# Decode attention over a 4096-token window: K and V in 4 MB slabs of 32 KB rows, five slots, in place of 2 MB slabs of 16 KB rows, eight slots

## The chip, the core and the metric

The kernel runs on one NeuronCore of a Trainium2 chip; the other cores are idle. The metric is the device time of one execution in microseconds (us). The profile adds, for one execution, the span from the first to the last instruction; it is about 2 us shorter than the measured time. Runs are called fast or slow by their state; only fast runs are compared, unless the text says otherwise. Ratios are the mean time of one kernel's fast runs over that of the other's of the same rounds, so they are not quite the ratio of the medians quoted beside them.

PE is the matmul engine, PEld its weight loads, DVE the vector engine, ACT the scalar engine, POOL the general engine, SP the engine that issues nearly all loads here. "Idle DMA" below is the time in which one of the core's 16 DMA engines has no packet, averaged over the 16; I summed it from the packet records of the trace, where each packet has a start, a duration and a size.

## The reference

Two independent problems A and B with the same shapes. One new token per batch attends to the last 4096 positions of a cache; two query heads share one kv head.

```python
B, Sq, D = 2, 1, 576
Hq, Hkv, Sk, Dh = 32, 16, 16384, 128
W = 4096
q = (x @ wq)                                   # wq: 576 x 4096
k = k_cache[:, :, Sk - W:, :]                  # each kv head serves 2 query heads
v = v_cache[:, :, Sk - W:, :]
p = softmax(einsum("bhqd,bhkd->bhqk", q, k) * Dh**-0.5)
o = einsum("bhqk,bhkd->bhqd", p, v)
out = o.reshape(B, 1, 4096) @ wo               # wo: 4096 x 576
# the outputs of A and B are joined along the last axis
```

All data are bf16. K and V windows are 134 MB, wq and wo 19 MB more, so 153 MB are read once.

## The kernel before

A slab is one kv head of both batches: 64 rows of 64 tokens for each batch, 128 partitions, 16 KB per partition, 2 MB. K and V slabs go through one ring of eight slots. SP issues all loads in one fixed order, the stream; it waits for each slot (or buffer) to be free, and everything behind waits too.

```python
NR = 8          # slots
LAG = 7         # V slab i stands behind K slab i + 7
for t in range(NSLAB + LAG):                      # NSLAB = 32
    if t < NSLAB:
        stream.append(("K", t))
    if t >= LAG:
        i = t - LAG
        if i % 4 == 0 and i // 4 < NG - 1:
            stream.append(("W", i // 4))          # a block of wo, 1.2 MB
        stream.append(("V", i))
stream.append(("W", NG - 1))
...
    # issue of a wo block: two buffers, so it waits for the projection before the last
    deps = [proj_op[i - 2]] if i >= 2 else []
```

For each K slab, DVE transposes 32x32 blocks (`xt`), then PE makes scores with a masked, shifted q as weights (`zq`). The scores of four slabs share two PSUM banks, so one softmax serves four slabs (eight softmaxes in all). The order of an iteration, which is the program order on each engine:

```python
make_X(t, 0); make_S(t, 0)        # DVE transpose of half a slab, 8 score matmuls on PE
make_chain(Gc)                    # every 4th t: max, transpose of it, bias, 4 exps
make_dg(Gp)                       # every 4th t: pick the diagonal of the PV product
make_X(t, 1); make_S(t, 1)
make_A(Gp); make_chain2(Gc); make_rl(Gp)
make_PV(i)                        # 16 matmuls, two 32-column tiles of PE at a time
make_chain3(Gc); make_evac(...)   # 1/sum, PSUM -> SBUF with that scale
make_proj(Gp)                     # times wo, summed in PSUM
...
```

## Time and profile before

| | before |
|---|---|
| time, median of the first three runs | 368.95 us (368.38 to 369.19) |
| span in the profile | 366.6 us |
| first packet / last data packet ends | 1.8 us / 363.3 us |
| idle DMA between | 1.8 us, 0.8 of it up to 345 us |
| PE, DVE busy | 74%, 51% |

From the page of the kernel before: the span, the busy times, the two rows of the 40 slices that concern the DMA (busy tenths, then GB/s), the packet sum, and four groups of instructions (busy us, mean ns of one, idle time before and its releaser). L437 is the transpose, L585 the PV product.

```profile
span 366.6 us, 3694 instructions
PE 271.8 (74%) x1700; PEld 101.0 (28%) x1435; DVE 185.9 (51%) x189; ACT 34.3 (9%) x114; POOL 14.1 (4%) x53
...
DMA  8999999999999999999999999999999999999994
GB/s 322 447 408 427 429 429 423 432 426 427 429 431 427 427 427 426 426 427 428 424 428 431 427 426 429 431 426 429 429 419 429 429 429 429 421 428 429 425 415 183
DMA packets 11264, 153.34 MB, mean 418 GB/s; under 512 B 1256, under 2 KB 1392, under 8 KB 2032
...
L437 DVE STREAM_TRANSPOSE xt<-ring 128x2048 f32<-128x2048 f32 x64 | 144.5, 2287 | 91.3 <-DMA ring<-in_A_k_cache_dram 46.7
...
L585 PE MATMUL ot<-ring,pT 128*32 128x512 bf16 x448 | 55.1, 395 | 0.7 <-ACT oE L610 0.7
...
ring<-in_A_v_cache_dram SPq DMA_DIRECT2D x16, 2048.0 KB, 35.8
...
wob<-in_A_wo_dram SPq DMA_DIRECT2D x4, 1152.0 KB, 33.5
```

The DMA engines are busy in every slice but the first and the last. A K or V load lands 33 to 37 us after SP issues it (medians of the page), because some 15 MB of loads are queued ahead of it. DVE idles for want of K. So this kernel is a stream of 153 MB with a short start and tail.

The queue's own waits (who SP waited for: us in total, times, longest) show that SP is blocked most of the time:

```profile
SPq L373 <- DVE xt L437: 133.4, 31, 8.1
SPq L373 <- PE ot L585: 45.4, 13, 4.5
SPq L347 <- PE pj L683: 43.5, 5, 10.4
```

L373 is the issue of a K or V slab, L347 that of a wo block, `pj` the projection.

### The profile page before, as it was taken

Reading aid. Unit: us, or ns where it says so; the run is one execution under the profiler, and the core shown is the slowest. Engines: PE = TensorE matmul, PEld = TensorE weight load, DVE = VectorE, ACT = ScalarE, POOL = GpSimd, SP = SyncE. Lnnn points to the kernel's source line nnn. Section 1 sums busy time; section 2 is a strip of 40 time slices with the busy share of each in tenths; the row PEclk is TensorE's granted clock in tenths of the full one; section 3 lists DMA queues with packets and bytes.
Section 4 is the critical chain, followed back from the end, with each engine's and each line's share of the span. In section 5 each row is a group of like instructions: output and inputs, shape, how many; then the busy total and the mean of one; then the engine's idle time right before and its main releaser. Section 6 shows DMA issues by size and latency. Waiting matters only on the chain.

```text
span 366.6 us, 3694 instructions
## 1 busy us (share of the span) xinstructions
PE 271.8 (74%) x1700; PEld 101.0 (28%) x1435; DVE 185.9 (51%) x189; ACT 34.3 (9%) x114; POOL 14.1 (4%) x53
## 2 busy tenths in 40 slices
PE   0635975987679788567968876794996677498797
PEld 0311112122214322132314321151223222143554
DVE  3104997967543674435744584407745476233100
ACT  1011002002000110002000020001200030002100
POOL 5010000000000000000000000000000000000000
PEclk9976897698985889895895998867798989958958
DMA  8999999999999999999999999999999999999994
GB/s 322 447 408 427 429 429 423 432 426 427 429 431 427 427 427 426 426 427 428 424 428 431 427 426 429 431 426 429 429 419 429 429 429 429 421 428 429 425 415 183
DMA packets 11264, 153.34 MB, mean 418 GB/s; under 512 B 1256, under 2 KB 1392, under 8 KB 2032
## 3 DMA queue, kind: packets, MB, share of 16 engines
q1 hardware_dynamic: 11236, 153.10, 98.6%
q8 instruction: 12, 0.20, 0.2%
q14 instruction: 4, 0.03, 0.0%
q10 hardware_dynamic: 12, 0.01, 0.0%
HBM read 153.10 MB, written 0.00 MB: 418 GB/s over the span
## 4 chain that ended last, share of the span: by engine, by line
DMA 82%; DVE 13%; PE 4%; SPq 0%; issue 0%
DMA ring<-in_B_k_cache_dram 41%; DMA ring<-in_A_k_cache_dram 28%; DVE xt L437 12%; DMA ring<-in_B_v_cache_dram 10%; DMA ring<-in_A_wq_dram 4%; PE ot L274 1%; PE st L461 1%; PE st L381 1%; PE pj L683 0%; PE st L395 0%; SPq L373 0%; PE st L594 0%; SPq L368 0%; DVE out_sb L693 0%; DVE ssum L536 0%
## 5 line engine op out<-in xcount | busy, mean ns | idle before, releaser
L437 DVE STREAM_TRANSPOSE xt<-ring 128x2048 f32<-128x2048 f32 x64 | 144.5, 2287 | 91.3 <-DMA ring<-in_A_k_cache_dram 46.7
L461 PE MATMUL st<-xt,zq 128*128 128x512 bf16 x256 | 115.6, 452 | 62.6 <-DVE xt L437 62.5
L381 PE MATMUL st<-xt,zq 128*128 128x512 bf16 x256 | 115.6, 451 | 0.0
L461 PEld LDWEIGHTS st<-xt,zq 128*128 128x128 bf16 x256 | 28.4, 111 | 158.8 <-DVE xt L437 82.7
L585 PE MATMUL ot<-ring,pT 128*32 128x512 bf16 x448 | 55.1, 395 | 0.7 <-ACT oE L610 0.7
L585 PEld LDWEIGHTS ot<-ring,pT 128*32 128x32 bf16 x448 | 20.5, 100 | 33.8 <-issue 15.4
L620 PEld LDWEIGHTS tb<-selv,oE 128*128 128x128 f32 x112 | 21.1, 280 | 5.8 <-issue 4.0
L620 PE MATMUL tb<-selv,oE 128*128 128x16 f32 x112 | 19.8, 324 | 0.8 <-ACT oE L610 0.8
L424 POOL TENSOR_TENSOR zq<-qs,bmask 128x64 bf16<-128x64 bf16 x32 | 9.2, 292 | 270.5 <-PE st L381 177.9
L639 DVE TENSOR_TENSOR oA<-tb,cmask 128x256 bf16<-128x256 f32 x7 | 3.0, 425 | 29.1 <-PE tb L620 29.1
L610 ACT ACTIVATE oE<-ot,rsb 128x512 f32<-128x512 f32 x14 | 9.6, 685 | 84.2 <-PE ot L585 84.2
L512 ACT ACTIVATE pR<-st,bias_sb 128x256 bf16<-128x256 f32 x32 | 15.9, 545 | 0.3
L471 DVE TENSOR_REDUCE mx<-st 128x2 f32<-128x512 f32 x16 | 10.0, 664 | 3.0 <-PE tb L651 3.0
L683 PE MATMUL pj<-wob,oP 128*2 128x288 bf16 x126 | 10.9, 324 | 0.3 <-ACT oP L655 0.3
L531 DVE STREAM_TRANSPOSE pT<-pR 128x512 bf16<-128x512 bf16 x16 | 10.4, 685 | 0.0
L501 PE MATMUL tb<-ones_f,nMrep 1*128 1x1 f32 x32 | 5.6, 276 | 6.0 <-DVE nMrep L495 6.0
L505 ACT ACTIVATE bias_sb<-tb 128x2 f32<-128x2 f32 x8 | 1.4, 172 | 89.1 <-PE tb L501 89.1
L255 PE MATMUL tb<-ident_b,xt 2*128 2x2 bf16 x36 | 2.3, 194 | 9.9 <-DVE xt L222 9.9
L655 ACT ACTIVATE oP<-tb 128x16 bf16<-128x16 f32 x8 | 1.5, 191 | 86.8 <-PE tb L651 86.8
L594 PEld LDWEIGHTS st<-pT,ring 128*128 128x128 bf16 x256 | 7.4, 102 | 5.1 <-DMA ring<-in_B_v_cache_dram 4.9
L594 PE MATMUL st<-pT,ring 128*128 128x16 bf16 x256 | 7.7, 173 | 0.5 <-DMA ring<-in_B_v_cache_dram 0.4
L631 DVE TENSOR_TENSOR oA<-st,cmr 128x64 bf16<-128x64 f32 x4 | 0.9, 225 | 13.7 <-PE st L594 13.7
(67 smaller groups left out, 92.7 us busy)
## 6 DMA issues: line engine op xcount, KB each, us to landing
ring<-in_A_k_cache_dram SPq DMA_DIRECT2D x16, 2048.0 KB, 33.2
ring<-in_A_v_cache_dram SPq DMA_DIRECT2D x16, 2048.0 KB, 35.8
ring<-in_B_k_cache_dram SPq DMA_DIRECT2D x16, 2048.0 KB, 37.1
ring<-in_B_v_cache_dram SPq DMA_DIRECT2D x15, 2048.0 KB, 36.9
ring<-in_A_wq_dram SPq DMA_DIRECT2D x1, 4608.0 KB, 13.8
ring<-in_B_wq_dram SPq DMA_DIRECT2D x1, 4608.0 KB, 24.3
wob<-in_A_wo_dram SPq DMA_DIRECT2D x4, 1152.0 KB, 33.5
wob<-in_B_wo_dram SPq DMA_DIRECT2D x3, 1152.0 KB, 30.8
```

What stands on the lines that cost most here:

```text
L381: return e.add_instruction(mybir.InstMatmult(name=nc.get_next_instruction_name(), engine=mybir.EngineType.PE, ins=[e.lower_ap(mv), e.lower ...
L424: return e.tensor_tensor(dst, src, msk, ALU.mult)
L437: Xop[(t, jb)] = S.add("dve", lambda e: e.transpose(xt[:, n % NXT, :].bitcast(FP32), ring[:, r, jb * HW_:(jb + 1) * HW_].bitcast(FP32)), d ...
L461: last = e.matmul(st[bk][:, 0:512], wt, mv, start=first, stop=True, skip_group_check=True)
L471: mxs = [S.add("dve", lambda e, jb=jb: e.tensor_reduce(mx[:, jb, :], st[jb][:, :].rearrange("p (x t) -> p t x", t=2), AX.X, ALU.max), [Sop ...
L512: last = e.activation(pR[:, jb, :].rearrange("p (x t) -> p t x", t=2)[:, t, :], st[jb][:, :].rearrange("p (x t) -> p t x", t=2)[:, t, :], ...
L531: chain[(G, "pT%d" % jb)] = S.add("dve", lambda e, jb=jb: e.transpose(pT[:, v, 512 * jb:512 * jb + 512].rearrange("p (w j q) -> p j w q", ...
L585: last = e.matmul(OTB[32 * c:32 * c + 32, :], pT[:, v, col:col + 32], ring[:, r, j * 128:(j + 4) * 128], start=(j % 32 == 0), stop=(j % 32 ...
L594: last = e.matmul(OL[m % 2][:, 0:16], ring[:, r, j * 128:(j + 1) * 128], pT[:, v, col:col + 16], start=(j == 0), stop=(j == KR - 1))
L610: evac_op[(G, pr)] = S.add("act", lambda e: e.activation(oE[:, pr, :], OTB[:, :], ACTF.Copy, scale=rsb[:, v, pr:pr + 1]), deps, "oE%d_%d" ...
L620: last = e.matmul(bank[:, 0:16], oE[:, pr, 128 * c:128 * c + 128], selv[:, pr, c, :], start=(pr == 0 and c == 0), stop=(pr == 1 and c == 3))
L683: last = e.matmul(PJ[half], oP[:, v, j, :], wob[:, v, j, half * NH:(half + 1) * NH], start=(proj_start(G) and j == 0), stop=True, skip_gro ...
```

## The change

Its intent is longer rows: a slab becomes four kv heads of one batch, interleaved on the partitions, 32 rows of 128 tokens each, so 32 KB per partition and half as many packets. A ring of five such slots takes 20 MB instead of 16, and only one wo buffer is kept. Each slab now holds 8 query rows by itself, so each has its own softmax, with four biases (one per kv head); PV uses all four column tiles of PE. The diff, cut to what matters:

```diff
-    NR = 8
-    NXT = 3
+    NR = 5
+    NXT = 5
-    LAG = 7
+    LAG = 2
-    KR = W // 64
+    KR = W // 32
-        wob = sb("wob", [128, 2, 8, NOUT], BF16)
+        wob = sb("wob", [128, 8, NOUT], BF16)
...
-                if i % 4 == 0 and i // 4 < NG - 1:
-                    stream.append(("W", i // 4))
+                if i % 2 == 1 and i // 2 < NSG - 1:
+                    stream.append(("W", i // 2))
                 stream.append(("V", i))
...
-                deps = [proj_op[i - 2]] if i >= 2 else []
+                deps = [proj_op[i - 1]] if i >= 1 else [q_free]
...
-            src = src_t[:, g, Sk - W:Sk, :].rearrange("b (r j) d -> r b (j d)", j=KR)
+            src = src_t[b, 4 * G:4 * G + 4, Sk - W:Sk, :].rearrange("g (r j) d -> r g (j d)", j=KR)
...
-                    for t in range(2):
-                        last = e.activation(pR[:, jb, :].rearrange("p (x t) -> p t x", t=2)[:, t, :], ...
+                    for t in range(4):
+                        last = e.activation(pR[:, bk, :].rearrange("p (x t) -> p t x", t=4)[:, t, :], ...
...
+                    for k in range(8):
+                        bk, jq = k // 4, k % 4
+                        for z in range(4):
+                            last = e.matmul(OTB[32 * z:32 * z + 32, :], pT[:, v, col:col + 32], ...
```

The iteration after the change, in program order (t is the K slab, c = t - 1 the slab whose softmax runs, i = t - 2 the slab whose PV runs, d = t - 3 the slab that is finished; `chain1` to `chain4` are the pieces of one softmax, and `dg`, `A` and `rl` pick the wanted part of a PV product and lay it out for the projection):

```python
make_X(t, 0); make_X(t, 1); make_S(t, 0)
chain1(c); make_X(t, 2); chain2(c); make_X(t, 3); make_S(t, 1)
make_dg(d); make_X(t, 4); make_X(t, 5); make_S(t, 2)
chain3(c); make_A(d)
if d % 2 == 1: make_rl(d // 2)
make_X(t, 6); chain4(c); make_X(t, 7); make_S(t, 3)
if d % 2 == 1: make_proj(d // 2)     # behind all 32 score matmuls of slab t
make_PV(i); make_evac(i)
```

## The prediction

> **What bounds it now.** The DMA stream. The page's slices show 16 busy DMA engines and 419 to 431 GB/s in nearly every slice between the start and the tail; 153.1 MB pass in about 358.4 us (first packet at 1.8 us, V cache landed near 360 us). The rest is a tail of some 6 us. PE is 74% busy, DVE 51%: both wait for data. The queue's own waits show SP blocked most of the time, but each load lands 33 to 37 us after issue, so some 15 MB are always queued and nothing starves.
>
> **What the change gives.** The packet records of the trace fit one line: 16 KB rows take 613 ns, 36 KB rows (wq) 1364 ns, 9.2 KB rows 352 ns, which is 436 GB/s over 16 engines plus about 12 ns per packet. This agrees with the Trainium skill, "DMA: Bandwidth & Descriptors", section "Where 436 GB/s comes from" (435 GB/s fabric ceiling). 32 KB rows halve the K/V packets: about 10,000 packets become about 6,000, so 4,000 x 12.2 ns / 16 = 3.0 us off the stream; the fewer completion writes give 0.2 us. PV on four column tiles shortens PE work (now 1.9 us per 2 MB slab), which is off the critical path. Start and tail keep their lengths. Best case: about 365.7 us, 1% faster.
>
> **What it adds.** Softmax runs 16 times, not 8, with eight short exps (estimate 0.37 us pitch from 0.475 us for twice the columns) and transposes of half the size (estimate 1.17 us each from a 2.24 us pitch). DVE grows by an estimated 35 to 40 us, still under 70%; this alone doesn't bind.
>
> **What I think binds.** wo now has one buffer, not two. The load of wo block n waits for projection n-1, and SP issues in order. That projection stands after all scores of the K slab that landed last but with only one V and one K slab queued behind it: 2 x 9.7 us = 19.4 us of cover. From landing to the end of that projection I chain, with durations of the trace: two transposes 2.4; scores 1.95 at full clock (3.4 to 3.9 at half); maximum transpose, nM, nMrep 0.9; next transpose 1.2; scores 1.95; dg 1.5; scores 1.95; row-sum transpose, ssum, rc, rs 1.2; last transpose 1.2; scores 1.95; projection 1.2: about 17.6 us at full clock. Issue to first data (1.0 to 1.2 us, seen at the start) and landing to consumer (0.5 us) leave no slack. PE has then been idle over 5 us. By the Trainium skill, "TensorE: Matmul & The Clock Gate", section "What's actually happening", an idle PE falls to half clock; the trace agrees (eight score matmuls take 1.75 or 3.39 us). With a cold first group the projection ends at 19.5 to 20.5 us: a bubble of about 1.8 to 2.8 us. It occurs six times (blocks 1 to 6): estimate 11 us in all, 0 to 20.
>
> **Prediction.** 368.95 - 3.2 + 11 = about 377 us; 80% range 366 to 387. Faster by over 2%: 3%; within 2%: 43%; slower by over 2%: 54%.
>
> **What would show it.** Right: K/V packets of about 1214 ns; DMA slices near 431 GB/s, with six dips some 43 us apart; in the queue's waits SP at the wo load waiting for the projection, and little else. Wrong: no dips (the stream alone, about 365 us); dips at K or V loads (compute loop too long); PV still 0.11 us per matmul.
>
> **What would make it wrong.** PE staying at full clock, or a shorter softmax chain, hides the wait; a colder PE (each score group +1.5 us) doubles it; 32 KB packets may not follow the line.

## The result, and the profile after

The changed kernel took 384.44 us (382.78 to 386.04, six runs) against 368.74 us for the kernel before in the same rounds: ratio 1.0423, 95% interval 1.0394 to 1.0452. It is 4% slower.

From the page of the changed kernel, the lines that answer to those above (L431 is the transpose, L552 the PV product, L491 the exps):

```profile
span 382.5 us, 3829 instructions
PE 238.2 (62%) x1613; PEld 89.5 (23%) x1353; DVE 218.1 (57%) x331; ACT 71.8 (19%) x322; POOL 9.7 (3%) x33
...
DMA  8999999999997999999997999769998999969994
GB/s 347 432 427 437 435 425 432 416 437 435 432 399 298 428 422 427 371 448 433 432 433 312 434 439 435 339 235 439 439 439 336 413 422 433 439 261 462 428 394 192
DMA packets 6802, 153.35 MB, mean 401 GB/s; under 512 B 760, under 2 KB 896, under 8 KB 1408
...
L431 DVE STREAM_TRANSPOSE xt<-ring 128x1024 f32<-128x1024 f32 x128 | 152.1, 1217 | 106.9 <-DMA ring<-in_A_k_cache_dram 54.0
...
L552 PE MATMUL ot<-ring,pT 128*32 128x512 bf16 x480 | 34.3, 408 | 0.3 <-DMA ring<-in_B_v_cache_dram 0.3
...
ring<-in_B_v_cache_dram SPq DMA_DIRECT2D x7, 4096.0 KB, 25.0
...
wob<-in_A_wo_dram SPq DMA_DIRECT2D x4, 1152.0 KB, 5.6
```

Six dips stand in the GB/s row (298, 371, 312, 235, 336, 261). PE and DVE are not near their limits. The plainest line is the last one: a wo block now lands 5.6 us after its issue, where it took 33.5 before. It is issued into a queue that has run empty.

The queue's own waits between 100 and 345 us leave no doubt who holds SP (L345 is the wo issue, L367 the K/V issue):

```profile
SPq L345 <- PE pj L633: 247.3, 6, 44.7
SPq L367 <- DVE xt L431: 0.6, 2, 0.5
```

The worst of the six, from the chain of waits (start us, length, what). The K slab landed at 229.74; the projection (`pj`) stands at 250.47:

```profile
229.74 2.38 DVE xt L431 x2
...
232.17 0.61 PE st L454
232.78 0.43 PE st L376
...
236.61 1.17 DVE xt L431
...
242.92 0.44 PE st L454
...
247.35 1.16 DVE xt L431
...
248.56 0.39 PE st L454
248.96 0.22 PE st L376
...
250.47 0.83 PE pj L633 x12
```

and SP's timeline just behind it:

```profile
251.58 0.33 SPq L345 DMA_DIRECT2D wob<-in_B_wo_dram  x1
251.96 0.54 SPq L367 DMA_DIRECT2D ring<-in_B_v_cache_dram  x1
252.54 0.60 SPq L367 DMA_DIRECT2D ring<-in_B_k_cache_dram  x1
253.19 0.64 SPq L367 DMA_DIRECT2D ring<-in_B_v_cache_dram  x1
253.87 0.65 SPq L367 DMA_DIRECT2D ring<-in_B_k_cache_dram  x1
```

The wo load comes 21.8 us after the landing; four slabs for which there had long been room go out within 3 us of it. The score matmuls (`st`) step by 0.43 us in the first three groups, which is half clock, and by 0.22 in the last. The DMA engines had run dry between 246.9 and 248.7, half of them by 247.1, and got data again from 252.55.

The other five are the same with other numbers. For the six wo blocks, the issue after the landing of the K slab whose scores stand ahead of the projection (the start of its first transpose), both from the timeline, and the idle DMA around it:

| wo block | 1 | 2 | 3 | 4 | 5 | 6 | sum |
|---|---|---|---|---|---|---|---|
| issue after landing, us | 19.5 | 18.1 | 18.1 | 21.8 | 19.3 | 19.1 | |
| idle DMA, us | 3.2 | 0.6 | 1.8 | 5.5 | 1.8 | 2.9 | 15.8 |

The bill: the last data packet ends at 378.5 us, 15.2 later than before (363.3). Idle DMA from the first packet to the last is 14.9 us more than before (16.7 against 1.8; the six gaps hold 15.8). The 9.2 KB packets of wo that restart the stream add about 3 us per engine (1024 of them sum to 25.6 us per engine, and to 22.5 us in the later runs where the queue never ran dry). The longer rows give back between 2 and 3 us. This sums to 15 to 16 us, so it closes within 1 us. From the last data to the end of the span it is 4.0 us, 3.3 before.

### The profile page after: what moved, and what is told of

Its sections match the earlier page's. It is cut to its first block, busy times and chain, and to the rows that moved or that the text cites. A ratio compares the mean times of both kernels' runs of the same rounds, so it can differ in the third digit from the quotient of the medians.

```text
span 382.5 us, 3829 instructions
## 1 busy us (share of the span) xinstructions
PE 238.2 (62%) x1613; PEld 89.5 (23%) x1353; DVE 218.1 (57%) x331; ACT 71.8 (19%) x322; POOL 9.7 (3%) x33
## 4 chain that ended last, share of the span: by engine, by line
DMA 57%; PE 21%; DVE 14%; ACT 4%; SPq 1%; issue 1%
DMA ring<-in_A_k_cache_dram 27%; DMA ring<-in_B_k_cache_dram 26%; DVE xt L431 9%; PE st L454 7%; PE st L376 7%; DMA ring<-in_B_v_cache_dram 4%; ACT pR L491 4%; PE pj L633 2%; PE ot L552 2%; DVE pT L510 2%; PE tb L577 1%; PE st L563 1%; SPq L367 1%; DVE nMrep L478 1%; DVE nM L475 1%
## 5 line engine op out<-in xcount | busy, mean ns | idle before, releaser
L431 DVE STREAM_TRANSPOSE xt<-ring 128x1024 f32<-128x1024 f32 x128 | 152.1, 1217 | 106.9 <-DMA ring<-in_A_k_cache_dram 54.0
L491 ACT ACTIVATE pR<-st,bias_sb 128x128 bf16<-128x128 f32 x128 | 47.9, 557 | 0.5
L491 ACT ACTIVATION_READ_ACCUMULATOR pR<-st,bias_sb 128x1 f32 x128 | 36.7, 286 | 0.0
L552 PE MATMUL ot<-ring,pT 128*32 128x512 bf16 x480 | 34.3, 408 | 0.3 <-DMA ring<-in_B_v_cache_dram 0.3
L465 DVE TENSOR_REDUCE mx<-st 128x4 f32<-128x512 f32 x32 | 20.0, 663 | 2.0 <-PE st L376 2.0
L510 DVE STREAM_TRANSPOSE pT<-pR 128x512 bf16<-128x512 bf16 x32 | 20.7, 685 | 0.0
L552 PEld LDWEIGHTS ot<-ring,pT 128*32 128x32 bf16 x480 | 16.8, 102 | 15.6 <-issue 7.5
L577 PE MATMUL tb<-selv,oE 128*128 128x8 f32 x120 | 16.8, 266 | 0.8 <-ACT oE L571 0.8
L533 PE MATMUL tb<-ones_f,rsrep 1*128 1x1 f32 x30 | 5.7, 256 | 16.7 <-DVE rsrep L523 16.7
L481 PE MATMUL tb<-ident_f,nMrep 4*128 4x4 f32 x32 | 6.5, 271 | 13.3 <-DVE nMrep L478 13.3
L418 POOL TENSOR_TENSOR zq<-qs,bmask 128x128 bf16<-128x128 bf16 x16 | 6.3, 399 | 302.4 <-PE st L376 285.0
```

The lines of the kernel that those rows point to most:

```text
L431: Xop[(t, k)] = S.add("dve", lambda e: e.transpose(xt[:, n % NXT, :].bitcast(FP32), ring[:, r, k * CW:(k + 1) * CW].bitcast(FP32)), deps, ...
L465: mxs = [S.add("dve", lambda e, bk=bk: e.tensor_reduce(mx[:, bk, :], st[bk][:, :].rearrange("p (x t) -> p t x", t=4), AX.X, ALU.max), [Sop ...
L481: n2, b2, bi = tb_job(lambda e, bank: e.matmul(bank[:, 0:4], nMrep[0:4].rearrange("o a q -> o (a q)"), ident_f[0:4, 0:4], start=True, stop ...
L491: last = e.activation(pR[:, bk, :].rearrange("p (x t) -> p t x", t=4)[:, t, :], st[bk][:, :].rearrange("p (x t) -> p t x", t=4)[:, t, :], ...
L510: chain[(s, "pT%d" % bk)] = S.add("dve", lambda e, bk=bk: e.transpose(pT[:, v, 512 * bk:512 * bk + 512].rearrange("p (z j q) -> p j z q", ...
L533: n4, b4, rb = tb_job(lambda e, bank: e.matmul(bank[:, 0:1], rsrep[0:1].rearrange("o a q -> o (a q)"), ones_f[0:1, 0:1], start=True, stop= ...
```

## The experiments

**Theory.** The loads are one in-order stream, and the single wo buffer ties it to a projection that stands late in the program. The queue drains while SP waits. **Rival 1.** The longer softmax chain (16 instead of 8) together with a PE at half clock sets the pace; the wait at wo is only where it shows. **Rival 2.** Five slots are too few. Every kernel below gave a correct result.

### E1: the wo load one step later in the stream

```diff
-                if i % 2 == 1 and i // 2 < NSG - 1:
-                    stream.append(("W", i // 2))
+                if i % 2 == 0 and i >= 2:
+                    stream.append(("W", i // 2 - 1))
```

> The changed kernel, with each wo block moved back in the order of the loads by one V and one K slab (it now stands before the V slab of the pair after next, still ahead of its projection). Buffers, slabs and compute are untouched. Theory (the wait of the wo load for the projection before it lets the stream run dry): cover behind the wait grows from 17-19 us to 37-39 us, the six gaps vanish, and what is left is the stream with 32 KB rows: 364 to 367 us, some 1% below before. Rival (the softmax chain per slab and a PE at half clock set the pace; the wo wait only shows it): the gaps move to K or V loads, the time stays within 2 us of 384. Second rival (five slots are too few): gaps stay too, with SP waiting at K or V loads.

Measured: 372.87 us (371.36 to 375.06), ratio to before 1.0126 (1.0099 to 1.0153). The six gaps are gone: idle DMA up to 345 us is 0.8 us, and the last data packet ends at 360.7 us, 2.6 us earlier than in the kernel before. Both rivals said that gaps would stay or move; they fell here. The time, though, missed the expectation by 6 us, because from the last data to the end it is now 9.9 us instead of 4.0. The slices show both, no dip and a dead end:

```profile
GB/s 323 442 424 451 417 431 449 415 433 413 450 426 424 442 421 437 424 435 420 442 432 424 434 421 442 423 428 426 437 437 421 442 421 440 424 423 433 411 309 2
```

### E2: the projection early, the stream untouched

```diff
             d = i - 1 if 1 <= i < NSLAB else None
+            if d is not None:
+                make_dg(d)
             if on:
                 make_X(t, 0)
...
                 chain1(c)
+            if d is not None:
+                make_A(d)
+                if d % Bb == 1:
+                    make_rl(d // Bb)
...
                 chain2(c)
+            if d is not None and d % Bb == 1:
+                make_proj(d // Bb)        # and its output, where a problem ends
...                                        # the same calls further down are removed
```

> The changed kernel, with the order of the loads untouched, but dg, its evacuation, rl and the projection of the slab pair that is finished moved from the end of the iteration to its start, so that they no longer stand behind the 32 score matmuls of the newest K slab. Theory: the wo load issues about 8 us instead of 19 us after the K slab landed, the queue keeps 9 to 11 us of cover, no gaps: 364 to 367 us, the same as with the load moved. Rival (softmax chain and cold PE set the pace): PE does the same work per slab, so within 2 us of 384.

Measured: 370.26 us (369.45 to 371.85), ratio 1.0048 (1.0030 to 1.0066). The wo loads are issued 8.1 to 9.6 us after the landing; idle DMA up to 345 us is 0.9 us:

```profile
GB/s 321 448 427 443 409 452 420 418 438 446 423 429 423 445 425 427 415 453 430 422 441 423 430 421 448 409 443 423 452 414 432 422 452 414 438 421 442 403 386 19
```

The time is 3 us above the range that was expected. PE and DVE do the very same work as in the changed kernel, wo has one buffer, the ring five slots, and the loads stand in the same order. Only the place of the projection, and of the steps that lead to it (`dg`, `A`, `rl`), in the program has changed, and 14 us came back. This settles the main question. Still in the queue's waits is

```profile
SPq L345 <- PE pj L633: 203.3, 7, 31.4
```

SP waits 203 us in total for the projection (177.8 of it between 100 and 345 us, where the changed kernel had 247.3) and loses nothing: what counts is how much is queued behind the wait, not how long it is.

Here too the tail is long, 7.6 us after the last data (360.9 us). The chain of waits shows why:

```profile
347.80 3.00 ACT pR L491 x16
...
350.99 1.21 DVE pT L510 x2
...
353.23 3.56 PE ot L552 x32
...
356.82 0.70 ACT oE L571
...
357.56 1.06 PE tb L577 x8
358.62 1.41 PE st L563 x56
```

The PV product of slab 14 (`ot`, 3.56 us) stands in PE's program behind the softmax of slab 15 (`pR`, `pT`), which it doesn't need. The first part of the last PV product (L563) starts only behind it, at 358.6. In the changed kernel this didn't show: V slab 14 landed so late (at 365.9 us; the product starts at 367.0) that the softmax of slab 15 was done by then. The gaps hid the tail.

### E3: E1 with 16 KB rows

Each slab is loaded as two transfers of half the columns; nothing else differs.

```diff
+                halves = [c0, c0 + 64, c1] if c1 - c0 == KR else [c0, c1]
...
-                    return e.dma_start(ring[:, r, c0 * 128:c1 * 128], src[:, :, c0 * 128:c1 * 128]).then_inc(sm, 16)
+                    for h0, h1 in zip(halves, halves[1:]):
+                        last = e.dma_start(ring[:, r, h0 * 128:h1 * 128], src[:, :, h0 * 128:h1 * 128]).then_inc(sm, 16)
+                    return last
...                                        # and the count of the loads to wait for
```

> The first run of this list (wo load later) with each 4 MB slab loaded as two transfers of 16 KB rows in place of one of 32 KB rows; slots, slabs and compute are the same. Theory: only the cost per packet comes back, 3968 more packets x 12 ns / 16 engines = 3.0 us more than the run with 32 KB rows, that is 367 to 370 us, level with before. If row length gives nothing, the two runs agree within 0.5 us.

Measured: 374.77 us (372.98 to 376.65), ratio 1.0170 (1.0141 to 1.0199), 1.9 us above E1. The expected time was missed by the same tail as in E1; the last data packet ends at 363.05 us against 360.69, so the rows are worth 2.4 us of stream here.

### E4: PE kept warm ahead of the landing

`heat(n)` is n needless matmuls of 512 columns into a free PSUM bank. PE is called warm while it runs at full clock (a score matmul every 0.22 us) and cold at half clock (every 0.43 us).

```diff
+                if t % 2 == 1 and 3 <= t <= 13:
+                    heat(20, "heat%d" % t)       # behind make_evac(i)
```

> The changed kernel with 20 needless matmuls (bf16, 512 columns, 4.3 us at full clock) on PE at the end of the iterations before those with a projection that a wo load waits for, where PE stood idle for 5 us or more. Theory with the clock part: the first score group after the landing then runs in about 1.9 us instead of 3.6 to 3.9 us, the projection ends 1.5 to 2.5 us sooner, and six gaps shrink by that: 9 to 15 us less than 384, so 370 to 376 us. If the clock has no part in it: 384 within 2 us, or more if the extra matmuls get in the way.

Measured: 385.98 us (382.94 to 387.56), ratio 1.0471 (1.0425 to 1.0516), no faster than the changed kernel, where 370 to 376 us had been expected. As a whole it tells nothing for or against the clock, because the extra work ended 2.1 to 3.2 us before four of the six landings, and PE cooled again. Single iterations of its trace do tell something. Where PE had been idle for 0.3 or 2.1 us when the first scores began (wo blocks 1 and 2), that group ran at full clock; where it had been idle for 4.6 to 5.6 us (3 to 6), at half. The first two score matmuls of blocks 2 and 3:

```profile
142.18 0.39 PE L454 MATMUL st<-xt,zq 128*128 128x512 bf16 x1 [2.05 <-DVE xt L431]
142.41 0.38 PE L376 MATMUL st<-xt,zq 128*128 128x512 bf16 x1
...
186.44 0.61 PE L454 MATMUL st<-xt,zq 128*128 128x512 bf16 x1 [5.50 <-DVE xt L431]
186.84 0.63 PE L376 MATMUL st<-xt,zq 128*128 128x512 bf16 x1
```

For block 1 all four groups ran at full clock: the wo load came 16.6 us after the landing, and idle DMA was 0.4 us. No other wo load of the changed kernel, of this one or of E5 came so early.

### E5: the same extra work ahead of the projection, and behind it

```diff
             if d is not None and d % Bb == 1:
+                if d <= 11:
+                    heat(8, "delay%d" % d)       # E5a
                 make_proj(d // Bb)
+                if d <= 11:
+                    heat(8, "delay%d" % d)       # E5b, in place of E5a
```

> The changed kernel with 8 needless matmuls (1.7 us at full clock, 3.4 at half) put on PE just ahead of each of the six projections that a wo load waits for. Theory (the wait for the projection sets the gaps): every gap grows by what is put ahead of it, 6 x 1.7 to 3.4 = 10 to 20 us, so 394 to 404 us; if they also warm the clock for the projection, a little less. Rival (PE and the softmax chain set the pace): the same growth, but then the next run must show it too.

> The changed kernel with the same 8 needless matmuls just behind each of the same six projections, ahead of the PV matmuls. Theory: the wo load no longer waits for them, so the gaps do not grow: 384 within 3 us. Rival (PE and the softmax chain set the pace): as slow as the run with the matmuls ahead of the projection, 394 us or more.

Measured: ahead of it 394.45 us (the median of three fast runs, 391.69 to 397.37; 395.91 with the slow one), ratio 1.0704 (1.0654 to 1.0754); behind it 385.75 us, ratio 1.0484 (1.0443 to 1.0526). The changed kernel had 1.0423 in its own rounds. So the same eight matmuls cost 2.8% of the kernel before, 10 us, ahead of the projection (1.7 us for each of six), and 0.6% behind it. This is what the theory asks for and rival 1 excludes.

The changed kernel, E4 and E5b together have 18 wo loads. A straight line through idle DMA against the issue after landing has a slope of 1.05 us per us and reaches zero at 16.8 us (correlation 0.95). The cover in this kernel is therefore about 16.8 us, and nearly every microsecond beyond it is lost.

### E6: E2 with the tail in a better order

In the iteration after the last K slab, PV of slab 14, its evacuation, dg and A move ahead of the wait for the softmax of slab 15.

```diff
+            if t == NSLAB:
+                make_PV(i)
+                make_evac(i)
             if c is not None:
                 chain3(c)
...
+            if t == NSLAB:
+                make_dg(i)
...
+            if t == NSLAB:
+                make_A(i)
             if c is not None:
                 chain4(c)
...                                        # the same calls elsewhere are skipped in this iteration
```

> The run with the early projection (370.3 us), and in its last iterations the PV product of the last slab but one, its evacuation, dg and A moved ahead of the wait for the softmax of the last slab. In that run the loads ended 2.4 us sooner than before, but 7.6 us instead of 3.3 us passed from the last data to the end: the PV product of slab 14 (3.6 us) stood behind the softmax of slab 15, which it does not need, then evacuation 0.7 and dg 1.1. Theory: those 4 us come back, 366 to 367.5 us, 0.3 to 0.7% below before. Rival (the tail is long for another reason, the needless matmuls between the last PV parts or the clock): 369 to 370.5 us.

Measured: 367.52 us (365.89 to 369.01), ratio 0.9978 (0.9953 to 1.0003); once more in other rounds (see E8) 367.99 us, ratio 0.9982 (0.9963 to 1.0000). So 2.3 to 2.7 us came back by the medians, not 4, and the runs scatter by 3 us; this kernel is level with the one before, not clearly below it. In the profiled run the tail was 3.9 us.

### E7: E6 with 16 KB rows

The edit of E3 on E6.

> The run before this in the list with each 4 MB slab as two transfers of 16 KB rows. Mean start-to-start of packets on one engine is 610.3 ns at 16 KB and 1212 ns at 32 KB in the traces so far, so 8.6 ns per pair of packets: 3968 x 8.6 / 16 = 2.1 us more than the run with 32 KB rows; the first estimate, 12.2 ns each, says 3.0 us. Level with before or up to 1 us above it. If the row length gives nothing, both runs agree within 0.5 us.

Measured: 370.71 us (368.68 to 371.54), ratio 1.0049 (1.0026 to 1.0072), against 0.9978 for E6 in the same rounds: 0.7%, 2.6 us. The last data packet ends 2.3 us later (363.1 against 360.9). The row length, alone, is worth this much. With 16 KB rows this version of the slab scheme is slower than the kernel before, even with the orders mended (1.0049); the version of E8 was not run with 16 KB rows.

### E8: E6 without the needless matmuls of the tail

The changed kernel, like the one before, ends with needless matmuls between the last PV parts and ahead of the last projection (nine here), to keep PE's clock up. The edit removes them:

```diff
-                filler(nf)
...
-        filler(1)
         make_proj(NSG - 1)
```

> The run with the early projection and the moved tail (367.5 us), without the nine needless matmuls between the last PV parts and before the last projection, which were there to hold the clock. In its trace PE works without a pause from 353.9 to 362.5 us, 3.1 us of it on these, and the last data came at 360.9. Theory (PE's program order sets the tail): the last part then waits for its data, and 0.5 to 1.5 us are gained: 366 to 367 us. Rival (they hold the clock): PE falls to half clock in the tail and the time stays or rises, 367.5 to 369 us.

> The run with the early projection and the moved tail once more, unchanged, beside the one without the needless matmuls and beside before: 366 to 368.5 us, ratio 0.995 to 1.000; is it below before by more than the noise?

Measured: 366.31 us (366.26 to 366.40), ratio 0.9940 (0.9927 to 0.9953), E6 beside it 0.9982. PE runs at half clock in the last projection (14 matmuls in 1.84 us), yet 1.7 us are gained and the scatter is gone. In the profiled run PE now waits for its data instead of working behind it. The timeline of this kernel, and then the last projection of E6's:

```profile
356.13 1.11 PE L563 MATMUL st<-pT,ring 128*128 128x16 bf16 x36 [0.69 <-DMA ring<-in_B_v_cache_dram]
358.02 1.40 PE L563 MATMUL st<-pT,ring 128*128 128x16 bf16 x36 [0.78 <-DMA ring<-in_B_v_cache_dram]
360.44 1.84 PE L632 MATMUL pj<-wob,oP 128*2 128x288 bf16 x14 [0.41 <-DMA wob<-in_B_wo_dram]
...
360.57 1.84 PE L633 MATMUL pj<-wob,oP 128*2 128x288 bf16 x14
```

So in E6's profiled run the needless matmuls had not held the clock either. Why the median fell by 1.7 us is not shown: the profiled runs of E6 (366.52 and 366.28 us, tails of 3.9 us) are level with that of E8 (366.40 us, 3.8 us). What is gone are E6's slower runs, of up to 369 us, and no trace of one of these was kept.

This version beats both kernels: 0.6% below before, 4.6% below the change as given (0.9940 against 1.0423, each over before).

## Why the prediction was right or wrong

**What bounds the kernel before: right.** DMA, without gaps.

**The gain of the rows: right in kind, a little too large.** K/V packets took 1213 ns where 1214 was predicted. The 12.2 ns per packet came from durations; consecutive packets on one engine overlap by a few ns (the DMA share in the stream is 1.01). Start to start they are 610.3 ns (16 KB) and about 1212 ns (32 KB), so a pair saves 8.6 ns, and 3968 pairs over 16 engines give 2.1 us, not 3.0. Counting the packets of the stretches that hold nothing but K and V gives 613.8 and 1218.0 ns, 9.6 ns for a pair and 2.4 us. The runs show 2.3 to 2.6 us.

**PV on four column tiles: right.** 32 matmuls of a 4 MB slab take 1.9 us, the time of the 16 matmuls of a 2 MB slab before (at full clock in both traces). The Trainium skill, "TensorEngine Tiling (Array Packing)", section "Theoretical Speedup", gives up to 4x for four tiles against one; this trace shows the factor of 2 between two tiles and four. It was worth nothing in time, as predicted: PE wasn't the limit.

**The cost of sixteen softmaxes: right.** DVE grew by 32 us (35 to 40 predicted), the exps step by 0.375 us (3.00 us for eight; 0.37 predicted), the transposes by 1.16 us (1.17). None of it binds; E2 has all of it and no gaps.

**The bubble at the wo load: right as a mechanism, and the term that was mis-sized.** Six gaps, 43 to 48 us apart, with SP at the wo load, were predicted and found; E1, E2 and the pair in E5 show the cause. The time was predicted at 377 us (366 to 387), and 384.44 was measured. The size of the gaps was 11 us predicted (1.8 each), 15.8 us of idle DMA measured (2.6 each), plus about 3 us of slow restart that the sum did not have. The time from the landing to the projection came out right by luck, because two errors in it cancelled. The steps were taken too long: with one score group cold I expected the projection to end at 19.5 to 20.5 us, and with one cold (wo blocks 2 and 3) the wo load came at 18.1; with none it came at 16.6 (E4, and two blocks of E1), 1 us earlier than my sum of durations said. But in the other blocks more ran cold than one group: a second group or the end of the chain (19.1 to 19.5), or three groups (21.8). The mean of the six is 19.3, no later than predicted. So what made the gaps larger is the cover. It was about 16.8 us and not the 17.7 that follow from two slabs (19.4) less the restart (1.2) and the landing (0.5), and 0.9 us six times over is about the 4.8 us that were missing. A likely reason is that the 16 engines don't run in step: in the example above half of them had run dry 17.4 us after the landing, the first at 17.1. That SP's wait holds all later loads fits the Trainium skill, "DMA: Bandwidth & Descriptors", section "Anatomy of one DMA — SWDGE (gpsimd) path", which says it of DMA in general: semaphore waits happen on the issuing sequencer, before dispatch, and not in the DMA engines. The trace agrees: 247.3 us of waits at wo loads, and four slabs issued within 3 us of the end of one.

**The clock: right.** The Trainium skill, "TensorE: Matmul & The Clock Gate", section "What's actually happening", lets an idle PE fall to half clock after an idle window of about 3.4 us. The traces fit: in E4 0.3 and 2.1 us of idle left PE warm and 4.6 to 5.6 us cold, and the stretches of one clock in the traces last 3.41 us or multiples of it. How long PE has just been idle doesn't decide it alone: the first group after the landing ran at full clock after 3.6 us in E1 (block 1) and at half after 2.7 us in E2 (block 4). That the clock alone sets the size of the gaps, as a cause, was not shown by a run of its own: E4 didn't keep PE warm. It is a reading of the single iterations.

**Start and tail keep their lengths: right for the kernel as given, wrong for the kernel without gaps.** The best case of 365.7 us assumed it. With the gaps removed the tail grew from 4.0 to 7.6 us (E2) and 9.9 us (E1), and it took E6 and E8 to reach 366.31 us.

## What to carry to other kernels

Where one engine issues all loads in order, a wait costs what the queue behind it can't cover: write down for each wait how many bytes are queued behind it, and when in the program its releaser runs. A buffer taken away to make room for larger tiles moves a wait; put its releaser early in the iteration, or the load later in the stream, before judging the larger tiles. When a gap is removed, look at the tail again, because gaps hide an unfavourable order at the end.

## What the Trainium skill lacked or had wrong

- "DMA: Bandwidth & Descriptors", section "Latency and other measured facts", gives about 0.6 us to the first byte of a load issued from SP, and does not say from where it counts. Here it was 1.0 us from the start of the issue, both at the start (issue at 0.8, first packet at 1.83) and after a dry queue (issue at 251.58, first packets from 252.55), and 0.6 us from the end of the issue, which itself takes 0.3 to 0.4 us. After a dry queue, the first 9.2 KB packets of wo took up to 1.5 us, against 0.35 us in a running stream; no page has this.
- "Perfetto Trace Analysis", section "DMA Optimizations", speaks of gains from under 2 KB up to 4 or 8 KB, and no page gives a gain beyond. From 16 KB to 32 KB rows, 2.3 to 2.6 us of 367 were still to be had (E3, E7), about 9 ns for each pair of packets made one.
- No page treats the cover behind an in-order wait: 178 us of waits cost nothing (E2), 247 us cost 15.8 us of idle DMA in the changed kernel, both between 100 and 345 us; the slope was 1.05 us per us beyond 16.8 us of cover.
- "TensorE: Matmul & The Clock Gate", section "HAM oscillation — how this bites in real kernels", has the rule of no PE-idle gaps over about 3.4 us. In the tail of this stream-bound kernel, the version without the matmuls that were to hold the clock was 1.7 us faster (E8; medians), and with them PE was at half clock in the last projection all the same (E6's profiled run).
